# Sliding-window attention with sinks and an RWKV channel mix on one core: two more units by DMA transpose, sink rows loaded directly, joint sink scores, and new hand-written orders

## The chip, the core and the metric

The program runs on one core of a Trainium2 chip. The core has five engines that each run their own instruction list in order: TensorE (PE in the profile; its weight loads are PEld), VectorE (DVE), ScalarE (ACT), GpSimd (POOL) and SyncE (SP), which here only starts transfers. Transfers are done by 16 DMA engines that work beside the five. The metric is the device time in microseconds of one execution of the whole program; less is better.

## The reference

Inputs are `q`, `k`, `v` of shape (4 batches, 8 heads, 768 positions, 64), two mixing vectors and three weight matrices, all float32. The output is float32 (4, 768, 512).

```python
scores = q @ k.T / sqrt(64)                      # per batch and head
keep   = (key < 4) | ((0 <= query - key) & (query - key < 128))
x      = softmax(where(keep, scores, -1e9)) @ v  # -> (B, S, 512), heads side by side
xk     = mu_k * x + (1 - mu_k) * x_prev          # x_prev: x one position earlier, 0 at the start
xr     = mu_r * x + (1 - mu_r) * x_prev
out    = sigmoid(xr @ w_r) * (relu(xk @ w_k) ** 2 @ w_v)
```

Each query sees the 128 positions up to itself and the first four positions of the sequence, the sinks. `w_k` is 512 x 1024, `w_v` 1024 x 512, `w_r` 512 x 512.

## The kernel before, in words

The work is cut into 12 **units** of 256 positions: unit u is batch u // 3, part T = u % 3. Every unit goes through four stages.

- **prepare** (lines 528 to 683): k and q come in as float32 in two halves each, are cast to bf16 (line 536 or 543) and turned so that the head dimension lies on the partitions. k of units 0 to 3 and q of units 0 to 7 are turned by TensorE (line 576) and copied out of PSUM (line 589). k of units 4 to 11 and q of units 8 to 11 are turned by a DMA transpose that SP starts (line 562): no PE and no copy. v is cast (line 646). In the first unit of a batch the sinks are set up too: GpSimd copies the keys of the four sinks into `ksink` (line 670), PE spreads the sink rows of v to the places where they are needed with a constant matrix `spread` (line 676), and DVE multiplies that by a head mask into `vsink` (line 680).
- **attend** (lines 686 to 831): PE makes the scores of two pairs of heads at a time (line 721), ACT takes the exponential (line 775), DVE applies the window mask (line 789), PE multiplies by the values (line 808), DVE divides by the row sums (lines 822 and 825) and so makes `x`. In parts 1 and 2 the sinks are added: PE makes their scores (line 696), ACT their exponential (line 703), PE their values (line 763).
- **mix** (lines 834 to 897): x is turned, for units 0 to 8 by PE (line 849) with a copy out of PSUM (line 858), for units 9 to 11 (the set `XD`) by two DMA transposes (line 869) into `xt`. DVE then makes `td`, the difference to the previous position (line 877), and from it the four column blocks of `xk` and the four of `xr` (line 888).
- **ffn** (from line 928): PE makes the keys product (line 939; 96 groups of four matmuls in all), ACT or DVE the relu and the square (lines 949 to 967), PE the gate (line 979, 24 groups) with a tanh on ACT (line 985), PE the product with `w_v` (line 997; the last piece line 909), DVE the gating (line 1006, the last 919), and SP the store (line 1013, the last 924).

No scheduler orders this at run time. Every piece of work is an entry of a plan, numbered as it is written down. Three constants order it: `ORDER` is the sequence in which the entries are issued, so that each engine's list is `ORDER` cut down to its own entries; `CHOICE` says which engine does an entry that can go to several (casts, copies, relu, square); `SLOTS` says which buffer each entry takes. Negative numbers in `ORDER` are matmuls on zeros (line 1018) that fill PE's early waits; there are 30. All transfers but two tiny ones are started by SP, in order, on one queue: a transpose whose cast isn't done holds up every transfer behind it. A load of k, q or v is 256 KB in float32, a weight load 1 MB, and a transpose moves a 128 x 512 tile of bf16, 128 KB.

The lists matter to what follows. On SP, the transfers that PE's first scores of unit 9 need end with the second transpose of q of unit 9, the 82nd transfer of the list; the transposes of x of unit 9 are the 97th and 98th. Of the 25 stores, 24 stand behind all loads. (Buffers `ob`, with the twelve quarters of the weight staging buffers, hold the finished rows until then.)

Of the kernel before, what the change touches and what calls it, by code (L numbers as in the profile page):

```python
# [8 lines left out]
FP32 = mybir.dt.float32  # L9
BF16 = mybir.dt.bfloat16  # L10
# [8 lines left out]
    92: "ACT", 93: "ACT", 94: "ACT", 95: "ACT", 97: "ACT", 100: "ACT", 102: "DVE", 105: "DVE",  # L19
    110: "DVE", 111: "DVE", 114: "ACT", 115: "DVE", 139: "POOL", 142: "POOL", 145: "POOL", 148:  # L20
    "DVE", 150: "DVE", 151: "ACT", 152: "ACT", 154: "DVE", 161: "DVE", 191: "DVE", 193: "DVE",
    194: "DVE", 197: "DVE", 199: "DVE", 200: "DVE", 203: "DVE", 204: "DVE", 213: "DVE", 230:
    "ACT", 234: "ACT", 273: "DVE", 276: "DVE", 279: "DVE", 282: "DVE", 285: "ACT", 286: "ACT",
    298: "DVE", 306: "DVE", 315: "ACT", 354: "DVE", 364: "ACT", 365: "DVE", 367: "DVE", 383:
    "ACT", 387: "ACT", 436: "DVE", 439: "DVE", 444: "DVE", 445: "DVE", 467: "ACT", 475: "ACT",
    514: "DVE", 516: "DVE", 521: "DVE", 524: "ACT", 525: "ACT", 546: "ACT", 550: "ACT", 554:
    "ACT", 558: "ACT", 595: "DVE", 598: "DVE", 603: "ACT", 604: "ACT", 606: "DVE", 634: "ACT",
    681: "DVE", 682: "DVE", 691: "DVE", 700: "ACT", 704: "ACT", 708: "ACT", 755: "DVE", 759:
    "DVE", 760: "ACT", 772: "DVE", 781: "ACT", 785: "ACT", 789: "ACT", 834: "DVE", 836: "DVE",
    837: "DVE", 853: "ACT", 856: "DVE", 857: "ACT", 860: "DVE", 861: "ACT", 904: "DVE", 906:  # L30
    "DVE", 910: "DVE", 912: "DVE", 913: "DVE", 929: "ACT", 933: "ACT", 940: "DVE", 941: "ACT",
    994: "DVE", 995: "ACT", 999: "ACT", 1003: "ACT", 1007: "ACT", 1022: "DVE", 1026: "DVE",
    1034: "DVE", 1035: "ACT",
# [5 lines left out]
XD = (9,10,11)  # L39
# [7 lines left out]
JOINT = ()  # L47
# [138 lines left out]
def kernel(  # L186
# [888 lines left out]
```

## Time and profile before

| what | value |
|---|---|
| time, median of 3 runs (lowest to highest) | 166.12 us (166.07 to 166.47) |
| the profiled execution: first to last instruction (its span) | 164.3 us |
| the profiled execution's own device time | not given apart from its span; the runs lie about 1.8 us above it |
| PE busy | 158.4 us, 96% |
| DVE busy | 145.4 us, 89% |
| ACT busy | 131.2 us, 80% |
| POOL busy | 13.5 us, 8% |
| packets of the main DMA queue, share of 16 engines | 86.3% |
| data moved | 34.60 MB |
| granted TensorE clock | 0.999 |

Columns of the views that are quoted below: in the groups by line, an engine, an operation, what it writes and reads, how often it occurs, then its busy time and the mean duration of one in ns, then the idle time before it. In the windows: the stretch, its length, the busy time and number of instructions of PE, PEld, DVE, ACT and POOL, the granted clock, the mean busy share of the 16 DMA engines (it passes 1 where packets overlap on an engine) and the GB/s moved. In the chain in order of time and in the timeline: start and length in us, then the engine and line; SPq is SP's issuing of transfers, whose length is the time of the issue and not of the transfer. In the DMA list: transfers by tile, their number, and the median time from issue to landing.

### The profile page before, as it was taken

The page shows a single profiled execution, that of the slowest core. Times are in us where ns is not written, and L with a number is a line of the kernel's source. Part 1 is how long each engine was busy: PE and PEld are TensorE (multiplying, and loading weights), DVE is VectorE, ACT ScalarE, POOL GpSimd, SP SyncE. Part 2 cuts the span into 40 slices and gives each one's busy share as a digit, 9 for nine tenths or more (in the row PEclk, how much of TensorE's full clock was granted, in tenths as well). Part 3 has the DMA queues.
Part 4 walks back from the last instruction along what each step waited for, and adds up shares of the span by engine and source line. Part 5 has one row for each costly group of instructions (what it writes and reads, how often), then busy time and mean ns, then how long its engine had stood idle before and what let it go on. Part 6 is the DMA issues. An engine that isn't in the chain of part 4 may idle for free.

```text
span 164.3 us, 4195 instructions
## 1 busy us (share of the span) xinstructions
PE 158.4 (96%) x1603; PEld 102.6 (62%) x1603; DVE 145.4 (89%) x381; ACT 131.2 (80%) x218; POOL 13.5 (8%) x38
## 2 busy tenths in 40 slices
PE   6999889999999999999999999999999999999992
PEld 2455568866467587577566775856575765664851
DVE  5259999999999999989999999999999999789752
ACT  3277999999999999999999999997668759163240
POOL 6409300010000000060000000000000000000000
PEclk9999999999999999999999999999999999999999
DMA  4999999999969896999999887986996955077743
GB/s 120 247 305 311 348 335 355 301 354 210 228 154 270 135 240 148 234 198 167 224 216 157 188 156 163 235 146 150 199 123 136 362 149 200 0 90 297 262 185 128
DMA packets 79042, 34.60 MB, mean 211 GB/s; under 512 B 67112, under 2 KB 73520, under 8 KB 79024
## 3 DMA queue, kind: packets, MB, share of 16 engines
q1 hardware_dynamic: 79008, 34.35, 86.3%
q8 instruction: 12, 0.20, 0.6%
q14 instruction: 6, 0.05, 0.1%
q10 hardware_dynamic: 16, 0.00, 0.0%
HBM read 24.12 MB, written 6.29 MB: 185 GB/s over the span
## 4 chain that ended last, share of the span: by engine, by line
PE 79%; ACT 8%; SPq 4%; DMA 3%; issue 2%; DVE 1%; POOL 1%; DVEq 0%; ACTq 0%; POOLq 0%
PE bank L997 23%; PE bank L939 23%; PE bank L979 12%; PE bank L808 6%; PE sc L721 6%; SPq L337 3%; DMA qs<-in_q_dram 3%; PE bank L576 2%; ACT e L775 2%; PE bank L849 2%; ACT rl L949 1%; PE bank L763 1%; ACT qt L589 1%; PE bank L909 1%; PE bank L1018 1%
## 5 line engine op out<-in xcount | busy, mean ns | idle before, releaser
L775 ACT ACTIVATE e<-sc 128x1024 bf16<-128x1024 f32 (+1 forms) x48 | 46.1, 994 | 1.8 <-PE sc L721 1.7
L939 PE MATMUL bank<-xk,wk_sb 128*128 128x256 bf16 x384 | 47.1, 273 | 0.0
L997 PE MATMUL bank<-wv_h,kk 128*128 128x512 bf16 x184 | 43.1, 379 | 0.1
L939 PEld LDWEIGHTS <-wk_sb 128*128 128x128 bf16 x384 | 36.4, 98 | 7.4 <-issue 0.4
L949 ACT ACTIVATE rl<-bank 128x512 bf16<-128x512 f32 x40 | 24.2, 625 | 8.6 <-PE bank L939 7.1
L997 PEld LDWEIGHTS <-kk 128*128 128x128 bf16 x184 | 17.1, 98 | 17.8 <-issue 0.4
L789 DVE TENSOR_TENSOR e<-e,mask 128x1024 bf16<-128x1024 bf16 (+1 forms) x40 | 25.4, 642 | 0.7 <-ACT e L775 0.5
L979 PE MATMUL bank<-wr_sb,xr 128*128 128x512 bf16 x96 | 23.7, 379 | 0.0
L888 DVE SCALAR_TENSOR_TENSOR xk<-td,mu_all,xt 128x256 bf16<-128x256 bf16 x48 | 22.4, 483 | 0.3
L888 DVE SCALAR_TENSOR_TENSOR xr<-td,mu_all,xt 128x256 bf16<-128x256 bf16 x48 | 22.1, 475 | 0.2
L967 ACT ACTIVATE kk<-rl 128x512 bf16<-128x512 bf16 x29 | 18.3, 664 | 4.2 <-DVE rl L953 4.0
L985 ACT ACTIVATE th<-bank 128x512 f32<-128x512 f32 x24 | 15.1, 646 | 5.7 <-PE bank L979 5.7
L825 DVE TENSOR_TENSOR x<-bank,rec 128x256 bf16<-128x256 f32 x48 | 19.2, 416 | 0.4
L808 PE MATMUL bank<-vb,e 128*128 128x65 bf16 x352 | 16.6, 194 | 0.0
L1006 DVE SCALAR_TENSOR_TENSOR w<-th,bank 128x512 f32<-128x512 f32 x19 | 13.0, 682 | 3.6 <-issue 1.8
L808 PEld LDWEIGHTS <-e 128*128 128x128 bf16 x352 | 13.6, 97 | 3.5
L979 PEld LDWEIGHTS <-xr 128*128 128x128 bf16 x96 | 8.8, 98 | 8.6 <-issue 0.2
L721 PE MATMUL sc<-qt,kt 64*128 64x128 bf16 (+1 forms) x256 | 13.9, 238 | 0.0
L721 PEld LDWEIGHTS <-kt 64*128 64x128 bf16 x256 | 8.9, 94 | 5.7 <-issue 3.1
L1018 PE MATMUL bank<-warm 128*128 128x512 bf16 x30 | 10.6, 484 | 1.1 <-DVE warm L1038 1.1
L877 DVE TENSOR_TENSOR td<-xt 128x512 bf16<-128x512 bf16 x24 | 10.3, 428 | 0.7 <-ACT xt L858 0.5
L589 ACT COPY qt<-bank 128x512 bf16<-128x512 bf16 x15 | 9.4, 643 | 1.0 <-PE bank L576 1.0
(74 smaller groups left out, 161.7 us busy)
## 6 DMA issues: line engine op xcount, KB each, us to landing
ks<-in_k_dram SPq DMA_DIRECT2D x24, 256.0 KB, 4.7
qs<-in_q_dram SPq DMA_DIRECT2D x24, 256.0 KB, 4.4
vs<-in_v_dram SPq DMA_DIRECT2D x24, 256.0 KB, 4.4
out_dram<-w SPq DMA_DIRECT2D x19, 256.0 KB, 2.7
w<-in_moe_w_k_dram SPq DMA_DIRECT2D x2, 1024.0 KB, 10.4
w<-in_moe_w_v_dram SPq DMA_DIRECT2D x2, 1024.0 KB, 9.3
w<-in_moe_w_r_dram SPq DMA_DIRECT2D x1, 1024.0 KB, 9.7
out_dram<-ob SPq DMA_DIRECT2D x4, 256.0 KB, 2.6
```

The lines of the kernel that those rows point to most:

```text
L721: nc.tensor.matmul(out=sc[:, a, o0:o1], lhsT=lhs[rows], rhs=rhs[rows], start=u not in BIAS, stop=True, skip_group_check=u in BIAS)
L775: nc.scalar.activation(out=buf[ek][:, :, lo:], in_=buf[sck][:, :, lo:], func=AF.Exp, scale=scale)
L789: nc.vector.tensor_tensor(out=at, in0=at, in1=m, op=ALU.mult)
L808: nc.tensor.matmul(out=o[:, g, a, :], lhsT=e[:, a, e0:e0 + 128], rhs=rhs, start=(T == 0 and i == 0), stop=(i == len(blocks) - 1), skip_gro ...
L825: P.op("DVE", dve(256), lambda ok=ok, rk=rk, c=c: nc.vector.tensor_tensor(out=buf["x", u][:, :, 128 * c:128 * c + 128].rearrange("p g (a d ...
L888: nc.vector.scalar_tensor_tensor(out=buf[key][:, c, :], in0=buf[tk][:, i, :], scalar=mu[w][:, c:c + 1], in1=xt[:, c, t0 - 1:t0 + 255], op0 ...
L939: nc.tensor.matmul(out=ps[:, i, :], lhsT=wk_sb[:, c, 128 * f:128 * f + 128], rhs=xk[:, c, :], start=(c == 0), stop=(c == NC - 1), skip_gro ...
L949: nc.scalar.activation(out=buf[rk], in_=buf[psk].rearrange("p (i t) -> p i t", i=2), func=AF.Relu)
L967: nc.scalar.activation(out=buf["kk", u][:, 2 * f2:2 * f2 + 2, :], in_=buf[rk], func=AF.Square)
L979: nc.tensor.matmul(out=buf[psk], lhsT=buf["xr", u][:, c, 128 * g:128 * g + 128], rhs=wr_sb[:, c, :], start=(c == 0), stop=(c == NC - 1))
L985: P.op("ACT", act(512), lambda psk=psk, tk=tk: nc.scalar.activation(out=buf[tk], in_=buf[psk], func=AF.Tanh, scale=0.5), rank + 4 + g, tak ...
L997: nc.tensor.matmul(out=buf[psk], rhs=wv_h[:, f, :], lhsT=buf["kk", u][:, f, 128 * g:128 * g + 128], start=(f == 0), stop=(f == NF - 1))
```

## The change

Four things are changed at once.

1. `XD` grows from units 9 to 11 to units 7 to 11. For units 7 and 8, four DMA transposes replace four groups of four PE transposes and four copies out of PSUM.
2. The sinks' rows of v no longer pass through PE. Four small transfers started by GpSimd at the beginning put the four sink rows of all batches and heads, in float32, into a new tile `vstage`, on partitions 16 h + i for head h and sink i. `vsink` is `vstage` times the head mask, on GpSimd (DVE for one batch). The matrix `spread`, its four matmuls and the four DVE products that read PSUM are gone; the column offset of the second head of a pair changes from 4 to 16.
3. `JOINT` takes in all four batches: the sink scores of a batch's units with T = 1 and T = 2 are made in one group of eight matmuls and one exponential of 512 columns, where there were two of four and two of 256. The unit with T = 2 is therefore prepared before the unit with T = 1 is attended.
4. `CHOICE`, `ORDER` and `SLOTS` are made anew.

What the new lists hold: casts of k and q on ACT / DVE / POOL go from 20 / 25 / 3 to 18 / 18 / 12, casts of v from 11 / 13 / 0 to 13 / 8 / 3, casts of `w_k` from 4 / 0 / 0 to 2 / 1 / 1, squares on ACT / DVE from 29 / 19 to 25 / 23. There are 26 filling matmuls where there were 30; two of them come after PE's first keys product. On SP, the transfers that the first scores of unit 9 need end with the second transpose of k of unit 9, now the 90th of the list. All of the 80 transfers that before ended with the first load of q of unit 10 are among these 90; the other ten are six loads (second halves of q and k of unit 10, second half of v of unit 9, first half of v of unit 10, first halves of q and k of unit 11), three transposes and one store. The transposes of x of unit 9 are the 111th and 112th; to the 98 of before come two loads of v, seven transposes (x of units 7 and 8, and three of unit 11) and five stores. On PE, the first keys product now comes behind the first scores of unit 2, and the scores of the later units come earlier among the products: ahead of the first scores of unit 11 PE has 64 keys, 16 gate and 30 value-product groups, where it had 76, 18 and 32.

```diff
-XD = (9,10,11)
+XD = (7, 8, 9, 10, 11)
-JOINT = ()
+JOINT = (0, 1, 2, 3)
 ...
+    vstage = tile1([128, B, D], FP32, "vstage")
 ...
-        for t, value in ((ones, 1.0), (spread, 0.0), (hmask, 1.0)):
+        for t, value in ((ones, 1.0), (hmask, 1.0)):
 ...
-        for t in ksink + vsink:
+        for t in ksink + vsink + [vstage]:
             nc.vector.memset(t, 0.0)
 ...
-            keep(m, -4 * a, [[-32, NP], [0, D + 1]], 1, m)
-            keep(m, 3 + 4 * a, [[32, NP], [0, D + 1]], -1, m)
+            keep(m, -16 * a, [[-32, NP], [0, D + 1]], 1, m)
+            keep(m, 3 + 16 * a, [[32, NP], [0, D + 1]], -1, m)
 ...
-    const_op("POOL", 200.0, make_spread, ["spread"], ["ident", "ones0"], rank=-54)
 ...
+    for i in range(NS):
+        P.op("POOL", 1000.0, lambda i=i: nc.gpsimd.dma_start(
+            out=vstage[i::16], in_=v[:, :, i, :].rearrange("b h d -> h b d")), -50,
+            service=60.0, descs=32, reads=["stage0"], writes=[("vstage", i)])
 ...
-                nc.gpsimd.tensor_copy(out=kz[rows, :, 4 * a:4 * a + NS],
+                nc.gpsimd.tensor_copy(out=kz[rows, :, 16 * a:16 * a + NS],
                                       in_=first(rows))
 ...
-        psk = ("vsp", b)
-        P.op("PE", 220.0, lambda: nc.tensor.matmul(
-            out=buf[psk].rearrange("p (h d) -> p h d", h=H), lhsT=spread,
-            rhs=buf["vb", u][:, 0, :, 0:D], start=True, stop=True), rank + 4, lag=PE_LAG,
-            take=[("bank", psk)], hold=[("vb", u)], reads=["spread", ("vb", u, 0)], writes=[psk])
-        P.op("DVE", dve(512), lambda: nc.vector.tensor_tensor(
-            out=vsink[b % 2][:, :, 0:D], op=ALU.mult, in1=hmask[:, :, 0:D],
-            in0=buf[psk].rearrange("p (h d) -> p h d", h=H)), rank + 4, hold=[psk],
-            reads=[psk, "hmask", "sinks"], writes=[("vsink", b % 2)])
+        def sink_values(engine):
+            return lambda: engine.tensor_tensor(
+                out=vsink[b % 2][:, :, 0:D], op=ALU.mult, in1=hmask[:, :, 0:D],
+                in0=vstage[:, b, :].unsqueeze(1).to_broadcast([128, H, D]))
+
+        P.op("POOL", 1250.0, sink_values(nc.gpsimd), rank + 4, port=True,
+             alts={"POOL": (1250.0, sink_values(nc.gpsimd), True),
+                   "DVE": (dve(512), sink_values(nc.vector), True)},
+             reads=[("vstage", i) for i in range(NS)] + ["hmask", "sinks"],
+             writes=[("vsink", b % 2)])
```

The constants `CHOICE`, `ORDER` and `SLOTS`, some 120 lines of numbers, are left out of this diff; what the prediction uses of them stands in the paragraph above it.

More of the change, by code (lines that the diff above doesn't have):

```diff
@@ L18 @@
 CHOICE = {
[L19 to L24, printed above, removed]
@@ L34 @@
+    930: "ACT", 981: "ACT", 982: "DVE", 985: "ACT", 986: "DVE", 989: "ACT", 990: "ACT", 993:
+    "ACT", 994: "ACT", 1009: "ACT", 1010: "ACT", 1013: "ACT", 1014: "ACT", 1017: "DVE", 1018:
+    "ACT", 1021: "DVE", 1022: "DVE",
 }
@@ L414 @@
     const_op("DVE", 500.0, fill, ["ones0"], rank=-80)
-    const_op("DVE", 1800.0, fill_later, ["sinks0", "ones", "edges"], rank=-79)
+    const_op("DVE", 1800.0, fill_later, ["sinks0", "stage0", "ones", "edges"], rank=-79)
     def keep(out, base, pattern, multiplier, in_=ones, fill=0.0):
@@ L446, in make_bias1 @@
         window_mask(early.bitcast(BF16)[:, 384:640], warm[:, 0:128], LOW)
-    def make_spread():
-        for a in range(2):
-            nc.gpsimd.tensor_copy(
-                out=spread[0:NS, :].rearrange("p (c w) -> p c w", w=32)[:, :, 4 * a:4 * a + NS],
-                in_=ident[0:NS, 0:NS].unsqueeze(1).to_broadcast([NS, NP, NS]))
     def make_hmask():
```

37 lines of the change are left out of this document (27 added, 10 removed), and 156 rows, old and new, of tables (ORDER, SLOTS).

## The prediction

> **What bounds the kernel now.** The page comes first, for the busiest engine and whether it is busy with work.
>
> ```profile
> PE 158.4 (96%) x1603; PEld 102.6 (62%) x1603; DVE 145.4 (89%) x381; ACT 131.2 (80%) x218; POOL 13.5 (8%) x38
> ```
>
> PE is nearly never idle. The chain in order of time says where the dense part begins and ends.
>
> ```profile
> 23.70 0.43 PE bank L1018 x2
> 24.13 0.90 PE bank L939 x8
> 25.03 0.22 PE bank L849 x4
> 25.25 0.22 PE bank L576 x4
> 26.47 0.55 PE sc L721 x12
> ...
> 51.95 0.22 PE bank L676
> ...
> 55.54 0.22 PE bank L696 x4
> ...
> 155.91 1.73 PE bank L979 x8
> 157.63 1.73 PE bank L997 x8
> 159.36 1.76 PE bank L909 x16
> 161.15 0.42 DVE w L919
> ```
>
> The last filling matmuls stand just before 24.1 us, then the first keys product; the last PE group ends at 161.15. The windows view gives that stretch and, in its last two columns, what the transfers do meanwhile.
>
> ```profile
> 5.00:40.00 35.00, 33.73 (x392) 22.52 (x391) 30.06 (x82) 30.66 (x49) 6.94 (x19) 1.00 1.05 313
> 24.00:161.00 137.00, 136.85 (x1388) 90.94 (x1387) 128.21 (x327) 114.88 (x193) 3.62 (x6) 1.00 0.87 200
> 39.30:100.30 61.00, 60.85 (x649) 40.32 (x646) 58.72 (x157) 60.27 (x106) 2.89 (x4) 1.00 0.95 194
> 39.30:118.80 79.50, 79.35 (x849) 52.17 (x846) 76.85 (x206) 76.43 (x133) 2.89 (x4) 1.00 0.95 189
> 80.00:85.00 5.00, 5.00 (x51) 2.67 (x49) 4.79 (x13) 5.00 (x11) 0.00 (x0) 1.00 1.18 219
> ```
>
> From 24 to 161 PE is busy 136.85 of 137.00 us at full clock: the program is a start of 24.1 us, 137.0 us of PE work without a hole, and 3.15 us of tail (161.15 to the span's end at 164.3). But the DMA engines are close behind: share 0.95 for the 61 us from 39.3, where the first stretch, which has nothing but loads to do, holds 1.05. A schedule that asks for transfers earlier asks this second resource for more, so the order on SP is read next, and the times from issue to landing.
>
> ```profile
> 13.56 2.66 SPq L354 DMA_DIRECT2D w<-in_moe_w_k_dram  x2
> ...
> 95.96 1.82 SPq L317 DMA_DIRECT2D qs<-in_q_dram  x1
> 97.88 2.52 SPq L562 DMA_TRANSPOSE qt<-qb  x2
> 100.45 0.57 SPq L317 DMA_DIRECT2D qs<-in_q_dram  x1
> 101.08 0.57 SPq L317 DMA_DIRECT2D ks<-in_k_dram  x1
> 101.69 0.89 SPq L307 DMA_DIRECT2D vs<-in_v_dram  x1
> 102.62 0.90 SPq L317 DMA_DIRECT2D ks<-in_k_dram  x1
> 103.70 1.70 SPq L562 DMA_TRANSPOSE kt<-kb  x1
> 105.44 0.58 SPq L317 DMA_DIRECT2D ks<-in_k_dram  x1
> 107.10 2.79 SPq L562 DMA_TRANSPOSE qt<-qb  x2
> 117.34 2.84 SPq L869 DMA_TRANSPOSE xt<-x  x2
> 121.54 0.57 SPq L1013 DMA_DIRECT2D out_dram<-w  x1
> ```
>
> ```profile
> kt<-kb SPq DMA_TRANSPOSE x16, 3.6
> xt<-x SPq DMA_TRANSPOSE x6, 3.5
> w<-in_moe_w_k_dram SPq DMA_DIRECT2D x2, 1024.0 KB, 10.4
> ```
>
> **The change, part by part.** *PE work.* The four groups of transposes of units 7 and 8 go: 4 x 0.22 (L849) = 0.9 us. Of the four spread matmuls, the three behind 24 us go: 3 x 0.22 (L676) = 0.7. The joint sink scores make one group of eight matmuls where there were two of four at 0.22 (L696). The trace has no such group; it lies between 0.22 (wholly side by side) and 0.44, and I take the middle, saving 0.1 for each of the three batches behind 24 us: 0.3. The new order puts one scores group (0.55, L721, and about 0.1 for the change of tile shape beside it) and one transpose group (0.22, L576) before the first keys product: 0.9. It keeps two filling matmuls behind it, 0.43 for two (L1018). Sum behind 24.1 us: -0.9 - 0.7 - 0.3 - 0.9 + 0.4 = -2.4; I use -2.3, which adding the new list up group by group gives. If PE stayed dense, 166.1 would become 163.8.
>
> *The start.* The first keys product waits for `w_k`: issued from 13.56 and 10.4 us to landing is 24.0, where it stands. The new SP list has 16 loads ahead of the weights, as before, so it stays. GpSimd gets four transfers there, of which no row shows the price; it is between nothing and the 1.25 us that SP needs for the dearest issue, a transpose (2.52 for two), so 0 to 5 us on POOL, with the casts of unit 1 behind them. I take nothing, since the weights cover it until 24; without that cover up to 2 us of it would reach PE.
>
> *VectorE, ScalarE, GpSimd.* In the dense stretch DVE is busy 128 of 137 us and ACT 115, and both lose work: seven casts of k and q and five of v leave DVE, two such and four copies out of PSUM leave ACT, and one of two exponentials per batch. It is covered by PE on all sides: priced at nothing. What moves goes to GpSimd (the last row gives least, median and longest of one in ns).
>
> ```profile
> L543 POOL CAST kb<-ks 128x512 bf16<-128x512 f32 x2 | 1.4, 702 | 0.0
> L536 DVE CAST kb<-ks 128x512 bf16<-128x512 f32 x6 | 2.5, 412 | 0.0
> L680 DVE TENSOR_TENSOR vsink<-bank,hmask 128x512 bf16<-128x512 f32 x4 | 2.7, 678 | 0.2 <-PE bank L676 0.2
> L877 DVE TENSOR_TENSOR td<-xt 128x512 bf16<-128x512 bf16 x24 | 10.3, 428 | 0.7 <-ACT xt L858 0.5
> L888 DVE SCALAR_TENSOR_TENSOR xk<-td,mu_all,xt 128x256 bf16<-128x256 bf16 x48 | 22.4, 483 | 0.3
> 70.30 2.54 POOL L670 COPY ksink<-kt 64x16 bf16<-64x16 bf16 x2 [36.96 <-DMA kt<-kb]
> L670 POOL COPY ksink<-kt x8: 188/196/2303, 16.2 to 96.6; 64x16 bf16<-64x16 bf16 x8
> ```
>
> Twelve more casts of v, k and q at 0.70, one of `w_k` of double size at 1.4, three products for `vsink` (no POOL row; at least DVE's 0.68, by the ratio of the casts, 702 to 412, 1.2 us): 13.4 us more on an engine busy 13.5 of 164. Hidden, unless a cast is held up: see the third rival.
>
> *Transfers.* This is where I expect the loss. The four added transposes cost SP 5 x 0.25 = 1.25 us each. But the reordering weighs more: PE attends later units earlier. Adding up the new PE list from 24.0, the first scores of unit 9 are due after 56 keys groups (0.90 for two at 24.13, 0.44 in a long run), 35 gate and value-product groups (0.86: 1.73 for two), 13 scores (0.54 or 0.65 with the change of shape) and the small ones, at 100.0 us; the first keys product of unit 9 at 125.4.
>
> Point one: the scores of unit 9 need 90 transfers done. With 3.6 us to land, the last must be issued by 96.4. In the trace SP finishes issuing the 80 that are common at 97.8 (95.96 + 1.82). Ten more follow: the ten from 97.88 to 109.89 took 12.0 us with five transposes; mine have three, so 11. At this pace the last is issued at 108.8, 12 us late.
> Point two: the keys product of unit 9 needs 112 transfers, and then two `td` and four `xk` on DVE, 2 x 0.43 + 4 x 0.48 = 2.8 us. So x must land by 122.6 and be issued by 119.1. In the trace 98 are issued at 120.2 (117.34 + 2.84). Fourteen more, seven transposes at 1.25, two loads and five stores at about 0.6 to 0.9: 13 us. Issued at 133.2, 14 us late.
>
> That is the upper end. The lower end is a DMA system that never idles. At share 1.05 instead of 0.95, the 69.5 us from 39.3 to 108.8 shrink to 62.9 and the 93.9 us to 133.2 to 85.0: still 5.8 and 5.2 us late. At 1.18, the best five microseconds quoted, 56.0 and 75.6: 1 and 4 us early. I take 7 us late, near the 1.05 case, because in the new list loads stand far ahead of their transposes, so SP should wait less for casts than it does now; above it, because transposes come in runs (five in a row, 5 x 1.25 = 6.3 us of SP for 3 to 4 us of data) that let the engines run dry. Nothing behind point two gives time back: PE's list is fixed, and what follows is PE work.
>
> Sum: -2.3 + 7 = +4.7, so a span of 169.0 against 164.3; the runs lie 1.8 above the span, 166.12 + 4.7 = 170.8.
>
> [...] The row: SP needs 2.52 us to issue two transposes of 128 KB each, against 0.57 for a load of 256 KB, and 3.6 us pass until one lands. [...] The row, in which the issue is the dear part, gives the 170.8 above.
>
> **The rivals.** *One, the other side: the queue keeps up, about 163.8.* If SP's waits for casts are what holds the share at 0.95, and loads issued well ahead end them, PE stays dense and the -2.3 us stand. It decides at a share of about 1.12: to issue the 90th by 96.4 the 69.5 us must shrink to 57.1, a share of 0.95 x 69.5 / 57.1 = 1.16, and 1.8 us more (1.12) still leave half a microsecond of gain; point two asks for 0.95 x 93.9 / 81.6 = 1.09 in the same way. For it: 1.18 occurs. Against it: over 35 us with loads alone 1.05 was all. A lag of 2 to 3 us would bring the old time back.
> *Two: the old pace, about 177.8.* If transposes themselves, not the waits, make the holes, the lag is 14 us: 166.1 - 2.3 + 14. For it: the share was 0.95 for 79.5 us, whatever stood in the queue. Against: loads now lead.
> *Three: GpSimd holds the queue, about 175.* Two tiny copies on POOL took 2.54 us at 70.30, one of them 2.30, where the median of such a copy is 0.2; DVE was dense there. Seven casts that feed transposes now run there; if each comes 2.1 us late (2.30 - 0.20) and two of the seven stop SP at a time when the queue is dry, 4.2 us are added to 170.8. Against it: these casts stand well ahead of their transposes. [...]
>
> **How the numbers follow.** My forecast, late transfers with 3 to 11 us of lag, 0.57; rival two 0.15; rival three 0.08; rival one 0.15; a lag that just eats the gain 0.05. So faster by over 0.3% (0.5 us, about what three runs that spread over 0.4 us can tell) 0.15, same 0.05, slower 0.80. The forecast's own range is 167 to 175; the range given runs from 163.5, just under rival one's 163.8, to 177.5, just under rival two.
>
> **What would show it.** Right: PE shows holes before L721 or before L808 and L939 with releasers kt<-kb, qt<-qb, vs or td, from some 80 us on and at most until 126; the DMA share from 40 to 118 above 1.0; the 90th transfer issued after 100 us; 0.9 us less of L849 and no L676. Wrong: PE busy without a hole to the end, or the last PE group before 160 us.

## The result: 5.2% slower, and where the profile after shows it

The changed kernel takes 175.11 us (median of four runs, 173.67 to 175.85); the kernel before, run beside it, 166.20. The ratio is 1.0519, with a 95% interval from 1.0464 to 1.0574. Medians in this document are over all runs of a kernel, while the ratios leave out the runs that are over 1.5% above its fastest. The profiled execution has a span of 174.1 us where the kernel before had 164.3. From the page of the changed kernel: the span, the busy times, the granted tensor clock in 40 slices, and the chain that ended last by engine; the last line is that chain in the kernel before.

```profile
span 174.1 us, 4156 instructions
PE 158.9 (91%) x1562; PEld 100.8 (58%) x1579; DVE 144.7 (83%) x369; ACT 128.0 (74%) x206; POOL 26.6 (15%) x56
PEclk9999999999999999999969999999999999999999
PE 40%; DVE 25%; DMA 13%; SPq 10%; ACT 5%; issue 5%; POOL 0%; DVEq 0%; ACTq 0%; POOLq 0%
PE 79%; ACT 8%; SPq 4%; DMA 3%; issue 2%; DVE 1%; POOL 1%; DVEq 0%; ACTq 0%; POOLq 0%
```

The chain is the first thing to read. Before, PE was 79% of what set the end; now it is 40%, and half of the chain runs through the vector engine, transfers and SyncE's queue. Nothing has become the new bound by being busy: DVE is busy a little less than before (144.7 against 145.4 us). PE is stopped, again and again, by things that come late. The clock line has one digit that is not 9; more of that below.

The windows view of the changed kernel, for a stretch that the prediction used and two parts of it (busy us and instructions of PE, PEld, DVE, ACT, POOL; then granted clock, DMA share, GB/s):

```profile
39.30:100.30 61.00, 54.83 (x558) 34.81 (x562) 52.85 (x134) 51.54 (x85) 6.87 (x12) 0.97 1.21 211
60.00:80.00 20.00, 16.61 (x193) 11.48 (x190) 17.67 (x42) 17.69 (x28) 3.50 (x6) 1.00 1.34 204
80.00:100.00 20.00, 17.38 (x167) 10.15 (x167) 15.42 (x42) 14.77 (x25) 0.61 (x1) 0.91 1.24 195
```

The last two stretches in the kernel before:

```profile
60.00:80.00 20.00, 19.89 (x234) 13.99 (x231) 18.67 (x52) 19.91 (x36) 2.50 (x2) 1.00 0.94 191
80.00:100.00 20.00, 20.00 (x211) 13.28 (x209) 19.49 (x52) 19.67 (x36) 0.39 (x2) 1.00 0.99 190
```

Between 39 and 100 us PE loses 6 us (54.83 of 61.00, before 60.85), 3.4 of them between 60 and 80. The DMA share goes from 0.94 to 1.34 there, and the bytes only from 191 to 204 GB/s. The transfer view of those 20 us gives the packets of the main queue, their MB and their share, first before and then in the changed kernel:

```profile
q1 hardware_dynamic: 13488, 3.76, 92.9%
q1 hardware_dynamic: 13593, 4.04, 133.1%
```

Nearly the same number of packets takes 1.4 times the summed time: each takes longer, and more of them overlap. So the share is no measure here of how fast the queue moves.

Who stopped PE, by the waits view of the changed kernel (us in total, times, longest), and how it came about, by the chain in order of time:

```profile
PE bank L989 <- ACT qt L598: 2.5, 1, 2.5
PE bank L773 <- ACT es L713: 1.7, 2, 1.4
PE bank L949 <- DVE x L835: 1.6, 2, 1.0
```

```profile
59.22 4.59 DMA ks<-in_k_dram
63.83 0.04 DVE kb L545
...
64.18 0.19 DVE rec L832
64.39 0.43 DVE x L835
...
64.86 0.60 PE bank L949 x4
...
77.29 3.35 SPq L571
...
80.69 3.77 DMA vs<-in_v_dram
84.48 0.03 ACT vb L655
...
85.00 0.61 ACT qb L552
85.62 0.71 ACT e L785
86.33 0.52 ACT kk L977
86.84 0.48 ACT qt L598
...
87.37 1.02 PE bank L989 x4
88.39 3.03 PE bank L1007 x8
```

This is the mechanism. Hardly any of PE's waits names a transfer (0.5 us at L706, for `qt`); they name ACT and DVE. But each of these engines works through its list in order, and in the list stands the cast of a load. At 63.8 DVE does the cast of a load of `k` that has just landed, and only then the `rec` and `x` for which PE waits. At 84.48 ACT does the cast of `v` (unit 6) that landed just then; behind it in ACT's list stand a cast, an exponential, a square and the eviction that frees a bank, so PE gets on at 87.4. The load was late because SyncE stood for 3.35 us at a transpose (L571) ahead of it.

The hole costs more than its length. Windows of the changed kernel around it:

```profile
86.00:88.00 2.00, 0.63 (x3) 0.29 (x3) 1.64 (x4) 2.00 (x5) 0.00 (x0) 1.00 1.06 271
88.00:90.00 2.00, 2.00 (x8) 0.81 (x7) 1.25 (x4) 2.00 (x5) 0.00 (x0) 0.66 1.18 203
90.00:92.00 2.00, 2.00 (x12) 0.91 (x12) 1.61 (x5) 0.64 (x3) 0.00 (x0) 0.50 1.21 225
```

After 2.5 us in which PE did next to nothing, its granted clock is 0.66 in the 2 us from 88 and 0.50 in the next 2, and from 92 to 94 it is 0.98; a pair of product groups (L1007, eight matmuls) that takes 1.73 us elsewhere takes 3.03 in the chain above. Behind the two next longest holes of the dense part, 1.40 us up to 61.66 and 1.01 up to 64.86, it stays at 1.00 in every 2 us from 60 to 70. That the hole of 2.5 us brings the half clock is the author's reading of this order; it was not tested by itself. The half clock is not in every run: the mean granted clock is 0.990 in the two runs of 175.8 us, and 0.996 and 1.000 in those of 173.67 and 174.41.

The transfers themselves, from SyncE's timeline of the changed kernel:

```profile
104.38 2.79 SPq L571 DMA_TRANSPOSE kt<-kb  x1
107.26 2.52 SPq L879 DMA_TRANSPOSE xt<-x  x2
...
129.01 3.25 SPq L879 DMA_TRANSPOSE xt<-x  x2
```

The first is the 90th transfer (the last that unit 9's scores need), the last row the 111th and 112th (x of unit 9). They are issued by 107.2 and 132.3.

### The profile page after: what moved, and what is told of

Same layout as the page of the kernel before. It is cut to its first block, busy times and chain, and to the rows that moved or that the text cites. A ratio compares the mean times of both kernels' runs of the same rounds, so it can differ in the third digit from the quotient of the medians.

```text
span 174.1 us, 4156 instructions
## 1 busy us (share of the span) xinstructions
PE 158.9 (91%) x1562; PEld 100.8 (58%) x1579; DVE 144.7 (83%) x369; ACT 128.0 (74%) x206; POOL 26.6 (15%) x56
## 3 DMA queue, kind: packets, MB, share of 16 engines
q1 hardware_dynamic: 81184, 34.88, 87.4%
## 4 chain that ended last, share of the span: by engine, by line
PE 40%; DVE 25%; DMA 13%; SPq 10%; ACT 5%; issue 5%; POOL 0%; DVEq 0%; ACTq 0%; POOLq 0%
PE bank L1007 15%; PE bank L949 11%; DMA ks<-in_k_dram 8%; PE bank L989 6%; SPq L348 4%; DVE xk L898 4%; DMA vs<-in_v_dram 4%; DVE x L835 4%; DVE e L799 4%; DVE xr L898 3%; PE bank L818 3%; SPq L571 2%; SPq L328 2%; PE sc L731 2%; ACT e L785 2%
## 5 line engine op out<-in xcount | busy, mean ns | idle before, releaser
L785 ACT ACTIVATE e<-sc 128x1024 bf16<-128x1024 f32 (+1 forms) x48 | 44.8, 959 | 1.7 <-PE sc L731 1.4
L1007 PE MATMUL bank<-wv_h,kk 128*128 128x512 bf16 x175 | 44.4, 388 | 0.5
L1007 PEld LDWEIGHTS <-kk 128*128 128x128 bf16 x184 | 17.3, 99 | 17.8 <-issue 1.3
L989 PE MATMUL bank<-wr_sb,xr 128*128 128x512 bf16 x88 | 23.2, 379 | 2.9 <-ACT qt L598 2.5
L898 DVE SCALAR_TENSOR_TENSOR xk<-td,mu_all,xt 128x256 bf16<-128x256 bf16 x48 | 23.6, 516 | 0.1
L898 DVE SCALAR_TENSOR_TENSOR xr<-td,mu_all,xt 128x256 bf16<-128x256 bf16 x48 | 23.4, 500 | 0.0
L995 ACT ACTIVATE th<-bank 128x512 f32<-128x512 f32 x24 | 14.3, 604 | 2.3 <-PE bank L989 2.2
L977 ACT ACTIVATE kk<-rl 128x512 bf16<-128x512 bf16 x25 | 15.5, 632 | 0.7 <-DVE rl L963 0.6
L655 ACT CAST vb<-vs 128x512 bf16<-128x512 f32 x13 | 8.0, 623 | 5.7 <-DMA vs<-in_v_dram 5.7
L832 DVE RECIPROCAL rec<-bank 128x4 f32<-128x4 f32 x48 | 7.9, 174 | 4.8 <-PE bank L818 4.5
L545 POOL CAST kb<-ks 128x512 bf16<-128x512 f32 x6 | 5.0, 826 | 40.6 <-DMA ks<-in_k_dram 28.5
## 6 DMA issues: line engine op xcount, KB each, us to landing
w<-in_moe_w_r_dram SPq DMA_DIRECT2D x1, 1024.0 KB, 11.2
```

The source lines that it names most:

```text
L785: nc.scalar.activation(out=buf[ek][:, :, lo:], in_=buf[sck][:, :, lo:], func=AF.Exp, scale=scale)
L898: nc.vector.scalar_tensor_tensor(out=buf[key][:, c, :], in0=buf[tk][:, i, :], scalar=mu[w][:, c:c + 1], in1=xt[:, c, t0 - 1:t0 + 255], op0 ...
L977: nc.scalar.activation(out=buf["kk", u][:, 2 * f2:2 * f2 + 2, :], in_=buf[rk], func=AF.Square)
L989: nc.tensor.matmul(out=buf[psk], lhsT=buf["xr", u][:, c, 128 * g:128 * g + 128], rhs=wr_sb[:, c, :], start=(c == 0), stop=(c == NC - 1))
L995: P.op("ACT", act(512), lambda psk=psk, tk=tk: nc.scalar.activation(out=buf[tk], in_=buf[psk], func=AF.Tanh, scale=0.5), rank + 4 + g, tak ...
L1007: nc.tensor.matmul(out=buf[psk], rhs=wv_h[:, f, :], lhsT=buf["kk", u][:, f, 128 * g:128 * g + 128], start=(f == 0), stop=(f == NF - 1))
```

## The experiments

Two theories were set against each other. **T**: the new order asks for transfers earlier than the queue can bring them; late loads block ACT and DVE through their casts, and so PE. **P**: the copies and products moved to GpSimd slow the vector engine. The expectations also speak of a *replay*: the written lists, each engine in its order, with durations from trace rows and with the transfers one after another at the service times that stand in the kernel's plan (1.25, 0.93 or 0.8 us, which no run measures by themselves; the 3.7 us for four transposes and some 10 us for eight loads come from them). Its figures are estimates.

| kernel | us (median) | ratio to before, 95% interval |
|---|---|---|
| after | 175.11 | 1.0519 [1.0464, 1.0574] |
| after, half of the load bytes | 167.45 | 1.0073 [1.0047, 1.0098] |
| after, GpSimd work left out | 175.96 | 1.0545 [1.0483, 1.0606] |
| after, both | 165.70 | 0.9967 [0.9931, 1.0003] |
| before, half of the load bytes | 166.00 | 0.9980 [0.9962, 0.9998] |
| after, SyncE's order made anew | 172.77 | 1.0382 [1.0335, 1.0430] |
| after, GpSimd work given to DVE | 174.96 | 1.0489 [1.0434, 1.0544] |
| after, x of 7 and 8 by PE again | 177.27 | 1.0582 [1.0522, 1.0641] |
| before + x of 7 and 8 by DMA | 172.54 | 1.0372 [1.0336, 1.0407] |
| before + v rows by GpSimd transfers | 165.86 | 0.9979 [0.9956, 1.0002] |
| before + 8 loads | 171.82 | 1.0335 [1.0294, 1.0377] |
| before + 8 transposes | 170.53 | 1.0220 [1.0138, 1.0303] |
| before + 24 GpSimd copies | 169.21 | 1.0187 [1.0148, 1.0227] |

### Half of the load bytes

```diff
+    def part(key):
+        return H if key[1] < 4 else H // 2
...
-                        out=buf[key][:, g, :, :],
-                        in_=v[b, :, s0:s0 + 128, :].rearrange("h p d -> p h d")), rank,
+                        out=buf[key][:, g, 0:part(key), :],
+                        in_=v[b, 0:part(key), s0:s0 + 128, :].rearrange("h p d -> p h d")), rank,
...
```

(and likewise for both forms of the loads of q and k)

> The changed kernel with the loads of k, q and v of units 4 to 11 cut to half of their heads (half of the bytes and of the packets of those transfers); every cast, matmul and transpose still runs on whole tiles, partly on older data, so the output is not the reference's. Theory T (the transfers come late, and casts that wait for them at the head of the in-order lists of ACT and DVE stop the tensor engine): the transfers regain their lead, the holes between 59 and 126 us go, and the kernel ends at about 163 to 165 us; the DMA share between 60 and 100 us falls from 1.3 to under 1.0. Theory P (copies on GpSimd slow the vector engine): nothing it depends on has changed, 174 to 175 us. Estimate by a replay of the written lists (each engine in its order, durations from the rows of both traces, one transfer after another with the service times written in the kernel's own plan; it gives 165.1 for the kernel before and 173.4 for the one after, profiled 164.3 and 174.1): 162.7 us.

Measured: 167.45 us, 7.7 less. The windows row of this kernel for the stretch in which the changed kernel had lost 6 us:

```profile
39.30:100.30 61.00, 59.52 (x651) 39.60 (x658) 60.05 (x152) 57.78 (x97) 11.43 (x15) 1.00 0.68 137
```

PE has 59.52 of 61.00 us again, at full clock, and the DMA share is 0.68. Theory T holds for the larger part of the loss. But 163 to 165 was expected, so 2.5 us or more are still there. The control, the same cut in the kernel before:

> Control: the kernel before with the same cut of its loads (half of the heads of k, q and v of units 4 to 11; the output is not the reference's). Its transfers have a margin, so nothing should come of it: 165.5 to 166.5 us (replay 164.9 against 165.1). If halved loads help by another way than the lead of the transfers (less work for the memory, another clock), it would be under 165.

Measured: 166.00 us, a ratio of 0.998. The kernel before gains next to nothing from cheaper loads, so the 7.7 us are not a general effect of moving less.

### The GpSimd work left out, alone and with halved loads

```diff
+SKIP = (282, 288, 414, 589, 645, 594, 643, 647, 524, 747, 821, 754, 875)
...
-            else:
+            elif i not in SKIP:
                 self.ops[i]["emit"]()
```

(the numbers are the casts q3.1, q5.1, k7.0, k7.1, q8.0, k8.0, k8.1, k9.1, k10.1, v11.0 and the three later writings of `vsink`)

> The changed kernel with both suspected causes taken away: loads of units 4 to 11 cut to half of their heads, and ten casts of GpSimd from unit 2 on and the writings of the sinks' v rows of batches 1 to 3 left out (what reads them finds older data, so the output is not the reference's). The kernel with the halved loads alone took 167.45 us, with 5.2 us of holes in the tensor engine's list where the kernel before has 2.2. If both causes add up (late transfers, and GpSimd copies that stretch vector instructions, which cost 2.9 us when 24 of them were put into the kernel before): 164 to 165.5 us. If GpSimd's share is small and the rest is the start or the order of the lists: 166.5 to 167.5.

> The changed kernel with full loads, but the same GpSimd work left out (ten casts from unit 2 on, the sinks' v rows of batches 1 to 3; the output is not the reference's). If the vector engine is only slowed where the tensor engine waits for a load anyway, the two causes overlap: 173 to 175 us. If they add up: 171.5 to 173.

Measured: with halved loads 165.70 us, 1.75 less than with halved loads alone; with full loads 175.96, no gain at all. So the two causes overlap: with full loads the vector engine's lost time is lost again in waits for loads. That there is such lost time is seen in DVE's busy time. With halved loads and the GpSimd work in place:

```profile
PE 155.8 (94%) x1562; PEld 100.1 (60%) x1579; DVE 145.7 (88%) x369; ACT 127.5 (77%) x206; POOL 28.8 (17%) x56
```

With that work left out, and the last PE group of its chain:

```profile
PE 155.3 (95%) x1562; PEld 100.1 (61%) x1579; DVE 140.3 (86%) x369; ACT 127.0 (78%) x206; POOL 16.5 (10%) x43
...
158.28 1.76 PE bank L927 x16
```

The same 369 DVE instructions take 5.4 us less when 13 GpSimd instructions are gone, 0.4 us for each of them; with full loads it is 3.5 us (144.7 to 141.2; in the window from 24 to 161 us 123.63 to 119.93, with 313 and 311 instructions), 0.3 us for each. Where this reaches PE can be read in the changed kernel, from the timelines of GpSimd, DVE and PE around two of the products for `vsink`:

```profile
74.10 1.29 POOL L685 TENSOR_TENSOR vsink<-vstage,hmask 128x512 bf16<-128x512 f32 x1
74.33 1.34 DVE L655 CAST vb<-vs 128x512 bf16<-128x512 f32 x1
77.86 0.27 PE L773 MATMUL bank<-vsink,es 64*128 64x130 bf16 x3 [0.85 <-DVE rl L963]
103.25 1.12 POOL L685 TENSOR_TENSOR vsink<-vstage,hmask 128x512 bf16<-128x512 f32 x1
103.35 1.30 DVE L898 SCALAR_TENSOR_TENSOR xk<-td,mu_all,xt 128x256 bf16<-128x256 bf16 x1
105.25 0.93 PE L949 MATMUL bank<-xk,wk_sb 128*128 128x256 bf16 x7 [0.59 <-DVE x L835]
```

The DVE instruction that meets such a product takes 1.3 us, where the cast takes 0.42 and the product for `xk` 0.48 elsewhere, and PE then waits for DVE.

The last PE group of this kernel ends at 160.04 (158.28 + 1.76). That is the list of the change without its burdens: 165.70 us, half a microsecond under the kernel before, by an interval that just reaches no change; 164 to 165.5 was expected.

### Only SyncE's order made anew

```diff
 # SyncE's list, by the plan's names, from the 36th on
-load k7.0, turn k4.0, turn k4.1, load k5.0, load v4.0, load v5.0, load k5.1, load q8.0, load k6.0, load k7.1, load v4.1, ...
+turn k4.1, turn k4.0, load v4.0, load k5.0, load k6.1, load k6.0, load v4.1, load k5.1, load q6.0, load q6.1, turn k5.0, ...
```

> The changed kernel with only the order of SyncE's list made anew, so that loads and transposes are issued in the order in which they are needed (v of units 4, 5 and 6 ahead of k of units 8 to 10, for example); the same transfers, and every other engine's list as it is. Theory T: the late loads come earlier and part of the lag goes: the replay gives 168.5 us, so 167 to 170; the bytes are the same, so it does not reach 164. Theory P: 174 to 175, since the copies on GpSimd stay. A third view, that the sum of the transfers alone is too large whatever their order: also 174 to 175.

In this kernel one filling matmul of the first 25 us comes ahead of the reading of one values bank of unit 0, so a part of that unit's output is not computed; the work and the waits behind are as described. Measured: 172.77 us, 2.3 less than the changed kernel, less than the 5 to 8 expected. The stretch from 39 us is nearly repaired (59.22 of 61.00, below), and the holes move to 100 to 120 us.

```profile
39.30:100.30 61.00, 59.22 (x644) 39.39 (x651) 58.79 (x152) 57.45 (x96) 8.09 (x12) 1.00 1.03 197
```

Every engine but SyncE runs the same sequence of operations as in the changed kernel. So the order of SyncE's list is a part of the loss, 2.3 us of it as tried here; with the other engines' lists as they are, the holes behind 100 us stay.

### GpSimd's work given to the vector engine

```diff
     CHOICE = {
-    282: "POOL", 288: "POOL", 414: "POOL", 524: "POOL", 589: "POOL", 594: "POOL", 643: "POOL", 645: "POOL", 754: "POOL",
+    282: "DVE", 288: "DVE", 414: "DVE", 524: "DVE", 589: "DVE", 594: "DVE", 643: "DVE", 645: "DVE", 754: "DVE",
```

> The changed kernel with the four writings of the sinks' v rows and the casts q3.1, q5.1, k7.0, k7.1, k8.0 and q8.0 taken from GpSimd and given to the vector engine, at their places in the order; GpSimd keeps little between 40 and 110 us. Theory P: the stretched vector instructions of 75 us (a cast of 1.34 us beside a GpSimd product, 0.42 elsewhere) go back to 0.42, and 1 to 3 us come back: 172 to 174. Theory T: the casts wait for the same loads, only on another engine, and the vector engine gets some 5 us more of work: 174 to 176 (replay 173.9 against 173.4).

(Of the four writings one was the vector engine's already, so three were moved.) Measured: 174.96 us against 175.11, no difference. That fits T. It does not refute that GpSimd costs DVE time, as the page of this kernel shows:

```profile
PE 158.9 (92%) x1562; PEld 100.7 (58%) x1579; DVE 144.9 (84%) x378; ACT 127.4 (74%) x206; POOL 19.1 (11%) x47
```

DVE has nine instructions more than in the changed kernel, by an estimate from rows above some 4.6 us of work (six casts at 0.42, three products at 0.68), and is busy for 144.9 us against 144.7: what it was given cost it about as much when GpSimd did it.

### x of units 7 and 8 by PE again, in the new order

```diff
-XD = (7, 8, 9, 10, 11)
+XD = (9, 10, 11)
```

(with the four groups and evictions entered in the lists and the four transposes taken out)

> The changed kernel with the DMA transposes of x of units 7 and 8 undone: four groups of tensor-engine transposes and ScalarE evictions at their places, four SyncE transposes fewer, all other lists as they are. If the four added transposes are what fills the transfer queue: 3.7 us of transfers go, and with a queue that is always behind the time falls by as much, to about 171 us. If it is the order that lets the transfers fall behind (they are already late at 60 us, long before the first of these transposes is issued at 104 us): no gain, 174 to 176 us (replay 174.5, against 173.4 for the changed kernel).

Measured: a ratio of 1.0582 to the kernel before, where the changed kernel has 1.0519, with intervals that overlap; so no gain, and no loss that is clear of noise. The four added transposes are not what makes the new order slow.

### The transposes alone, in the old order

```diff
-XD = (9,10,11)
+XD = (7, 8, 9, 10, 11)
...
-xT u7.0, xevac u7.0, xT u7.1, xevac u7.1   (tensor engine and ScalarE; the same for u8)
+xturn u7.1, xturn u7.0                      (SyncE, behind the last x of the unit)
```

> The kernel before with the first part of the change alone: x of units 7 and 8 by four SyncE transposes instead of four tensor-engine groups and four evictions, each transpose at the first place behind the last piece of x, and the td, xk and xr of these units moved behind them; every other list as in the kernel before. Theory T (a transfer queue with a margin, which the new order has used up): 3.7 us of transfers more, some of them on the path, since a transpose lands 3.5 us behind its issue and SyncE holds the loads behind it: replay 169.1, so 167 to 170. If the parts of the change are harmless and only the new order costs: 165 to 166.5.

Measured: 172.54 us, 6.2 more than before. In the old order the transposes are dear, and more so than expected. From this kernel's SyncE waits, its chain, and its windows:

```profile
SPq L865 <- DVE vb L642: 5.8, 2, 3.1
```

```profile
102.93 0.73 SPq L558
103.72 3.50 DMA qs<-in_q_dram
107.24 0.43 DVE qb L532
```

```profile
100.00:120.00 20.00, 16.16 (x180) 10.11 (x178) 15.72 (x43) 14.76 (x25) 0.00 (x0) 1.00 0.87 164
```

SyncE stands at the transposes of x for work of DVE (5.8 us at two of them; before, 2.8 at one), the loads behind them go out late, DVE waits for one of these until 107.24, and PE has 16.16 of 20 us. The DMA share is 0.87, where the kernel before has 1.02 in this stretch and PE is busy for all 20 us: here it is the waiting of the in-order queue, not its throughput. What lands late counts too: PE waits 1.4 us for `xk` and 1.0 us for `xr`, which are made from the transposed x.

### More transfers in the old order: eight loads, eight transposes

```diff
+    spare = [const.tile([128, H, D], FP32, name=f"spare{i}") for i in range(3)]
+    for i in range(8):
+        P.op("SP", 600.0, lambda i=i: nc.sync.dma_start(
+            out=spare[i % 3], in_=v[i % B, :, 0:128, :].rearrange("h p d -> p h d")), 0)
```

> The kernel before with eight loads of 256 KB more on SyncE, of v rows that nothing uses, spread between 33 and 104 us (every 8 us or so): some 10 us of transfer service more, 7% of what it has. Theory T: the kernel before has a margin of about 5% in its transfers, and beyond that every microsecond of transfers is a microsecond of time: replay 171.1, so 168 to 172. If transfers are hidden (the kernel is bound by its tensor engine, and loads are issued far ahead): 166 to 167.

Measured: 171.82 us, 5.5 more than before. The chain that ended last in this kernel:

```profile
PE 47%; ACT 17%; DMA 16%; SPq 10%; DVE 4%; issue 3%; POOL 1%; DVEq 0%; ACTq 0%; POOLq 0%
```

It resembles the changed kernel's: PE 47%, transfers and SyncE's queue 26% (there 40% and 23%), though ACT stands here where DVE stood there. The kernel before, whose PE had no hole, was only a few transfers away from them: 2.1 MB more cost 5.5 us.

```diff
+    spare = [const.tile([128, NC, 128], BF16, name=f"spare{i}") for i in range(3)]
+    for i in range(8):
+        P.op("SP", 1240.0, lambda i=i: nc.sync.dma_start_transpose(
+            out=spare[i % 3], in_=wk_sb[:, 0, 0:512]), 0)
```

> The kernel before with eight DMA transposes more on SyncE (128x512 bf16 of the finished w_k into a tile that nothing reads, 128 KB each), at the very places where eight loads of 256 KB were put in and cost 5.5 us (171.82 against 166.32). It prices a transpose against a load, apart from any change of order or of who waits for it. If a transpose is a transfer like any other, half the bytes of such a load at the same speed: about half of the loads' cost or less, 166.5 to 169 us (the first part of it may vanish in the margin). If the issue (2.5 us for two, against 0.57 for a load) is the dear part, a transpose costs what a load does or more: 171 to 174. Replay, with 0.93 us of service and 1.2 us of issue each: 168.6.

Measured: a ratio of 1.022 with an interval from 1.0138 to 1.0303, so 2.3 to 5.0 us for eight transposes at the places of the loads (4.9 to 6.3 us by the loads' interval). The expectation's first case, half of the loads' cost, some 2.8 us as an estimate from the measured 5.5, lies inside; as dear as a load lies at the very edge. By the two ratios a transpose that waits for nothing costs about two thirds of a load of twice its bytes, with an interval that reaches from under a half to the whole. Four would then cost some 1.8 us by an estimate from this, so the 6.2 us in the experiment above are mostly the price of waiting at them and for them; that part is argued and not measured by itself.

### The sinks' v rows alone, in the old order

```diff
-        P.op("PE", 220.0, lambda: nc.tensor.matmul(
-            out=buf[psk].rearrange("p (h d) -> p h d", h=H), lhsT=spread,
...
+    for i in range(NS):
+        P.op("POOL", 1000.0, lambda i=i: nc.gpsimd.dma_start(
+            out=vstage[i::16], in_=v[:, :, i, :].rearrange("b h d -> h b d")), -50,
...
```

> The kernel before with the second part of the change alone: the sinks' v rows by four GpSimd transfers at the start, vector products from them, and no spreading matmuls; the vector engine keeps the four products at their places, the rest of every list is as before. Four matmuls of 0.22 us and one PSUM bank use each go from the tensor engine; replay 164.4 against 165.1, so about 165.5 us, 0.3 to 0.5% under the kernel before. If the four early transfers hold the first loads or the masks of GpSimd up, the first keys come later and it is 166 to 168.

Measured: 165.86 us, ratio 0.9979 [0.9956, 1.0002]: 0.5 us under the kernel before, run beside it, with an interval that just reaches no change. This part is harmless, and not yet shown to be a gain.

### Copies on GpSimd in the old order

```diff
+    spare = const.tile([128, 512], BF16, name="spare16")
+    for u in range(U):
+        for g in range(2):
+            P.op("POOL", 600.0, lambda u=u, g=g: nc.gpsimd.tensor_copy(
+                out=spare, in_=buf["th", u, g]), 0, hold=[("th", u, g)], reads=[("th", u, g)])
```

> The kernel before with 24 copies more on GpSimd (each th tile, 128x512 f32 to bf16, into a tile that nothing reads), 15 us of GpSimd work between 30 and 160 us, about what the change added there. Theory P: a copy on GpSimd takes the vector engine's time: its instructions beside these copies stretch by up to 0.6 us each, 24 of them up to 14 us, and the kernel ends at 168 to 175. Theory T: the tensor engine does not notice, 166 to 167 (replay 165.1 against 165.1).

Measured: 169.21 us, 2.9 more, for work that nobody needs and that no instruction is shown to wait for. From this kernel's page, its groups and GpSimd's timeline:

```profile
PE 159.1 (95%) x1603; PEld 102.4 (61%) x1603; DVE 150.5 (90%) x381; ACT 131.7 (79%) x218; POOL 33.6 (20%) x62
L1041 POOL CAST spare<-th 128x512 bf16<-128x512 f32 x24 | 21.8, 910 | 104.7 <-ACT th L985 104.4
```

```profile
70.28 4.14 POOL L1041 CAST spare<-th 128x512 bf16<-128x512 f32 x2 [11.82 <-ACT th L985]
```

DVE's 381 instructions take 5.1 us more than before (150.5 against 145.4), and the copies are uneven: 0.91 us in the mean and 4.14 for two at 70.28, where the shortest takes 0.61. So DVE was slower with the copies beside it, and some copies were slow; by what means, no row shows. T had expected nothing here and was wrong: a dense PE hangs on DVE closely enough to feel 5 us.

## Why the prediction came out as it did

The forecast was 170.8 us, slower, with a range up to 177.5; 175.11 lies in the range, 4.3 above the forecast and just above the forecast's own 167 to 175. That it lies inside is owed to the upper end, which rival two set by the old pace of the transfers. The steps, in the prediction's order:

- *PE work, -2.3 us: right.* In the list without burdens (halved loads, GpSimd work left out) the first keys product stands at 25.4 and the last PE group ends at 160.04: 134.6 us, where the kernel before had 137.0 from 24.1 on. The 2.4 us are saved in the changed kernel too, whose PE list is the same. The group that no row had shown, the joint sink scores, takes 0.33 us there (L706 at 58.34, the next group at 58.67), the middle that was taken.
- *The start, priced at nothing: wrong by 1.1 us in the profiled execution.* The four GpSimd transfers took 2.3 us of GpSimd together, within the 0 to 5 given. The cover that was named, the landing of `w_k`, still stands; but SyncE issued it at 14.34 us instead of 13.56, behind the same 16 loads, and ACT's first cast of it came 1.2 us later. From the timelines, three rows of the changed kernel and ACT's cast in the kernel before:

```profile
14.34 3.56 SPq L365 DMA_DIRECT2D w<-in_moe_w_k_dram  x2
24.02 1.08 ACT L510 ACTIVATE wk_sb<-w 128x1024 bf16<-128x1024 f32 x1
25.15 1.05 PE L949 MATMUL bank<-xk,wk_sb 128*128 128x256 bf16 x8
...
22.85 1.08 ACT L501 ACTIVATE wk_sb<-w 128x1024 bf16<-128x1024 f32 x1
```

  In the profiled executions of the kernel before and of seven kernels with the new lists, the first keys product stands 10.4 to 10.8 us behind that issue (issues from 12.91 to 14.67 us, first keys from 23.70 to 25.40). The issue time scatters by over a microsecond although the seven have the same first loads. What moves it was not tested, and PE had other work up to its first keys product, so the 1.1 us are not explained beyond this.
- *VectorE and GpSimd, 13.4 us more on GpSimd, "hidden": the size right (13.1), the price wrong.* The work is off GpSimd's own critical path but not off DVE's: 13 such instructions cost DVE 3.5 to 5.4 us. That cost 1.75 us of time with halved loads and 2.9 us when 24 copies were put into the old order. In the changed kernel PE waits behind it too, but leaving the work out gains nothing there. The third rival had GpSimd stop SyncE, whose waits name GpSimd for 0.6 us in all; what it slows is DVE.
- *Transfers, 7 us late: the mechanism right, the size too small, and the place wrong.* The 90th transfer was issued by 107.2 and the 112th by 132.3, near the old pace of 108.8 and 133.2 and not near the 103.4 (96.4 + 7) and 126.1 (119.1 + 7) that the forecast comes to. Scores of unit 9 ran at 111.22 and its keys at 137.39, 11.2 and 12.0 us behind the sums, of which 1.1 is the start. The step that failed is the conversion of the share into a pace: the prediction shrank the time by 0.95 / 1.05, and the share rose as far as 1.34 while the bytes rose by 7%. Its reason, that SyncE would wait less for casts, came true: the stretches of over 0.3 us without an issue from 39.3 us to the 90th transfer sum to 4.9 us before and 1.5 us after. Yet with 30 transfers issued by 39.3 us in both kernels, 81 were issued by 100.3 before and 84 after: the waits were not what held the pace. The range's other end, rival two at the old pace, had the transfers right; it gave 177.8 since it counted 14 us of lag.

  Nor did the lag arise at the two points. It was nearly complete at 92 us, in a few holes from 59 us on; the larger ones stand behind loads of v, q and k whose casts stand in the in-order lists of ACT and DVE. The sum of transfers due at two late points gave the right order of size because the queue was behind all the way; who would stand waiting, and when, it could not tell. "What would show it" asked for holes with transfers as releasers from 80 us; the releasers named are ACT and DVE, and one has to go up the chain to find the load.
- *The price of a transpose, 1.25 us of SyncE for each: not what decided.* The rows show 1.26 (2.52 for two), and no parts of 0.25. Measured by themselves eight cost 2.3 to 5.0 us, where eight loads cost 4.9 to 6.3; but no price of a transpose would have given the time, since without the four added ones the new order was no faster (a ratio of 1.0582 against 1.0519).

The account in spans, 164.3 to 174.1: 1.1 us later at the start, 2.4 less PE work (from 25.2 to 170.66 there are 145.5 us where the unburdened list needs 134.6), 10.9 of holes and slow clock, 0.3 of tail (9.9, with rounding). In single profiled executions, halving the loads takes 7.6 of the 10.9 away (PE ends at 162.93, from first keys at 25.0) and leaving out the GpSimd work the other 3.3; the medians of all runs say 7.7 and 1.75 us.

Since PE's list is the same in all these kernels, two traces can be laid side by side by the starts of PE's weight loads, and the steps in which one falls behind the other can be read off. Against the list without burdens, the changed kernel loses 0.7 us by 31 us, 3.2 from 59 to 67, 1.1 at 77, 2.7 in the hole that begins at 84.9, 1.6 by the half clock behind it, 0.7 at 104 and 0.9 from 124 on. With halved loads alone three larger steps are left, of 0.9, 0.7 and 1.0 us, each within 5 us behind a product for `vsink`. With the GpSimd work left out and full loads, the steps at 31, 77 and 104 are gone, but the hole at 83 us lasts 3.3 us instead of 2.5 and the half clock behind it about twice as long (a mean granted clock of 0.94 over the 61 us from 39.3, where the changed kernel has 0.97), so nothing is gained. Of the 10.9 us, then, 7.5 are late loads and the half clock that follows them, and 2.5 are GpSimd's products; the last 0.9 are there without the GpSimd work too, and not with halved loads.

The cause of the whole, then, is the new order, with the GpSimd work that its `CHOICE` brings: with the x transposes undone it still costs 9.7 us by the ratio, and the v rows alone cost nothing in the old order. The joint sink scores were not tried alone, but they were in the list without burdens, which costs nothing. The transposes of x cost 6.2 us in the old order, and in the new one taking them out gains nothing; why they do not add to its loss was not followed up. Which features of the order are to blame (units attended earlier, loads of k far ahead of v, casts early in the lists) is settled only so far: SyncE's order accounts for 2.3 us of it.

## What to carry to other kernels

A kernel whose tensor engine has no hole can be a few transfers away from being bound by them (here eight loads more cost 5.5 us): price a reordering by the time at which each transfer is due, and follow each late load to the in-order engine whose next instruction is its cast, because everything behind that cast waits too. Read bytes per second, not the share of busy DMA engines, as the pace of a queue: here the share rose from 0.94 to 1.34 and the bytes from 191 to 204 GB/s. Work put on GpSimd was not free beside a dense vector engine; in these kernels it cost 0.2 to 0.4 us of vector time for each instruction, so a cast of 0.42 us taken from the vector engine gains little.

## What the runs showed of the hardware that was not expected

- Behind a hole of 2.5 us in PE the granted clock was 0.66 and 0.50 in two windows of 2 us and 0.98 in the next, about 3.5 us at half speed by an estimate from these three: a late transfer can be paid for twice. Behind the longer hole of the kernel with the GpSimd work left out and full loads, it was about 7 us, by an estimate from the mean of 0.94 over 61 us. Behind holes of 1.0 to 1.4 us, two in the changed kernel and three in the kernel before with x of 7 and 8 by DMA, it stayed at 1.00 (in windows of 2 us from 60 to 70, and over the whole profiled execution).
- A GpSimd copy or product of 0.6 to 1.3 us takes about 0.4 or 0.3 us from DVE (5.4 or 3.5 us for 13 instructions) or 0.2 (5.1 for 24), 0.8 to 0.9 us where a product for `vsink` meets one DVE instruction (1.30 against 0.48, 1.34 against 0.42), and can itself take long: the longest copy took 3.1 us, where the shortest took 0.61.
- Between 60 and 80 us the DMA share rose from 0.94 to 1.34 for 7% more bytes (3.76 to 4.04 MB) in about as many packets (13488 and 13593).
